# Batch 0 of a fused attention and max-out kernel reordered, its fill counted differently, its last tile split

## The chip, the cores and the metric

The kernel runs on one core of a Trainium2 chip. TensorE (PE) does matmuls and transposes into PSUM, ScalarE (ACT) and VectorE (DVE) read PSUM and write SBUF, GpSimd (POOL) works on SBUF and issues the loads that change type, SyncE (SP) issues plain loads and stores. Each engine works through its own instructions in the order in which the program names them. The metric is the device time of one execution in microseconds; lower is better.

## The reference

Blockwise causal attention, then a max-out layer:

```python
# q, k, v: [8 batches, 8 heads, 576, 64] float32; blocks of 64 positions
scores = scale * q @ k.transpose(0, 1, 3, 2)
scores = where(block_i >= block_j, scores, -1e9)      # block_i = pos // 64
attn = softmax(scores)                                # along the last axis
x = (attn @ v).transpose(0, 2, 1, 3).reshape(4608, 512)
g = maximum(x @ w1, x @ w2)                           # w1, w2: [512, 1024]
out = g @ w_out                                       # w_out: [1024, 512]
```

## The kernel before

The order of every engine's work is written out by hand (`manual_schedule`); a tile pool with `bufs=n` makes the (n+1)th tile wait until the first is done with.

*Attention.* The 64 heads are worked in 32 pairs, one per step `s`, four steps to a batch (`HP` = 4). Q and K come for two pairs at a time, as group `g` of 16: `load_qk` (float32, on SP's queue; group 0's K on ACT's), `cast` to bf16 on an engine that the call names, `transposes` on PE, and copies into `qT`, `kT`. With `gated=True` POOL first writes one column of the raw tile, and SP's load waits for that. A pair's scores come in two bursts. `burst_a` makes two PSUM tiles `u0`, `u1` and exps both on ACT, `burst_b` does so with `u2`, `u3`; the pool `ps_s` has two buffers, so `u2` waits for the exp of `u0`, and `u3` for that of `u1`. POOL zeroes the masked corners (`mask`). `av` multiplies a pair's exps with V and divides by the sums on DVE; a pair is 30 matmuls, 6 for row tiles 0 and 1 and 24 for 2 to 4. It runs `LAG` = 2 steps behind the scores. `x_out(g)` transposes the result of two pairs into `xT`; after a batch's second one `done_tokens` grows by 576.

*Max-out.* `xT` is taken in nine spans of 512 tokens. `h_unit` is 8 matmuls of 512 columns (four for w1, four for w2), a copy and a maximum on DVE; `y_unit` is 8 matmuls against `w_out`, a copy on ACT and a store on SP. They form one generator, `moe()`, of single matmuls. `fill(n)` takes the next n of them, as far as `done_tokens` allows: so they fill PE between the attention's steps. `fill_of(s)` spreads what is ready over the steps left until the batch after next:

```python
left = 10 - s if s < 10 else 4 - (s - 2) % 4
return -(-ready() // left)
```

`w1`, `w2`, `V` and `w_out` are loaded by POOL with a cast, through a queue of their own (q0 in the profile; SP's is q1).

*Order around the change.* In the main loop a step does: `n = fill_of(s)`; the `x_out` that is due; `burst_a`; part of the fill; the next group's transposes; `burst_b`; `pool_work(s)` (loads and casts ahead); `av(s - 2)` with fill between its parts; the rest of the fill. In steps 0 to 3 nothing is ready to fill, and `PLAN` puts `av(0)` at the end of step 2 and `av(1)`, `av(2)`, `av(3)` at the end of step 3. Step 4 first makes room for the transposes of group 2 and starts the fill.

Of the kernel before, what the change touches and what calls it, by code (L numbers as in the profile page):

```python
# [8 lines left out]
FP32 = mybir.dt.float32  # L9
# [5 lines left out]
def kernel(  # L15
# [10 lines left out]
    nc = tc.nc  # L26

    B, H, S, D = q.shape
    P = 128
    BLK = 64  # L30
    HP = H // 2
    NPAIR = B * HP
    d_model = H * D
    d_ff = moe_w1.shape[1]
    NDM = d_model // P
    NFF = d_ff // P
    NTOK = B * S
# [6 lines left out]
    RPP = S // NP  # L44
# [8 lines left out]
    NCH = 5  # L53
# [5 lines left out]
    ring = ctx.enter_context(tc.tile_pool(name="ring", bufs=1))  # L59
    small = ctx.enter_context(tc.tile_pool(name="small", bufs=4))  # L60
    xpool = ctx.enter_context(tc.tile_pool(name="xp", bufs=3))
    raw = ctx.enter_context(tc.tile_pool(name="raw", bufs=2))
    qkn = ctx.enter_context(tc.tile_pool(name="qkn", bufs=2))
    h1_pool = ctx.enter_context(tc.tile_pool(name="h1", bufs=3))
    g_pool = ctx.enter_context(tc.tile_pool(name="g", bufs=2))
# [23 lines left out]
    def load_qk(g, queues, gated=False):  # L89
        b, u = divmod(g, GPB)  # L90
        for nm, src, queue in (("q", q, queues[0]), ("k", k, queues[1])):
            raws[nm, g] = t = raw.tile([P, 2, RPP * D], FP32, name=f"{nm}raw")
            if gated:
                nc.gpsimd.memset(t[:, 0, :1], 0.0)
            queue.dma_start(
                out=t[:],
                in_=src[b, 4 * u:4 * u + 4].rearrange(
                    "(s h) (p t) d -> (h p) s (t d)", h=2, t=RPP),
            )

    def cast(nm, g, parts):
        t = raws.pop((nm, g)).rearrange("p s (t d) -> p t s d", d=D)
        qk_n[nm, g] = n = qkn.tile([P, RPP, 2, D], BF16, name=f"{nm}n")
        for copy, j0, j1 in parts:
            copy(out=n[:, j0:j1], in_=t[:, j0:j1])  # L105

    def load_v(b, c):
        rows = min(P, S - c * P)
        nc.gpsimd.dma_start(  # L109
            out=vv_r[b % NV][:rows, c, :, :D],  # L110
            in_=v[b, :, c * P:c * P + rows, :].rearrange("h p d -> p h d"),
        )
# [5 lines left out]
    def load_w(f0, fw):  # L118
        for dst, src in ((w1_sb, w1r), (w2_sb, w2r)):
            nc.gpsimd.dma_start(out=dst[:, :, f0:f0 + fw], in_=src[:, :, f0:f0 + fw])  # L120

    def load_wo(c0, n):
        nc.gpsimd.dma_start(out=wo_sb[:, c0:c0 + n, :], in_=wor[:, c0:c0 + n, :])
# [16 lines left out]
        nc.vector.memset(aT_r[r][BLK:, :, CB[4] + 512:], 0.0)  # L140
        nc.vector.memset(aT_r[r][:BLK, :, AW:], 0.0)
    cast("q", 0, ((dve, 0, 6), (pool, 6, RPP)))
    cast("k", 0, ((act, 0, 6), (pool, 6, RPP)))
    for c in range(3):
        load_v(0, c)
    cast("q", 1, ((pool, 0, RPP),))
    for c in range(3, NCH):
        load_v(0, c)
    load_w(0, 256)
    load_w(256, 256)  # L150

# [26 lines left out]
    def y_unit(i, s):  # L178
        g = g_tiles[i]
        t0 = i * SPAN + s * P  # L180
        py = ps_m.tile([P, d_model], FP32, name="ps_y", tag="m")
        for f in range(NFF):
            nc.tensor.matmul(  # L183
                py[:], g[:, f, s * P:(s + 1) * P], wo_sb[:, f, :],
                start=(f == 0), stop=(f == NFF - 1),
            )
            if f == NFF - 1:
                y = y_pool.tile([P, d_model], FP32, name="y")
                nc.scalar.copy(out=y[:], in_=py[:])  # L189
                nc.sync.dma_start(out=out[t0:t0 + P, :], in_=y[:])  # L190
            yield

    def moe():
        ny = SPAN // P
        for i in range(NSPAN):
            need = (i + 1) * SPAN
            for f in range(NFF):
                yield from ((need, 0) for _ in h_unit(i, f))
                if i > 1 and f % 2 == 0:
                    yield from ((need, 0) for _ in y_unit(i - 1, f // 2))  # L200
            if i == 0:
                for s in range(ny):
                    yield from ((need, 0) for _ in y_unit(0, s))
        for s in range(ny):
            yield from ((NTOK, 0) for _ in y_unit(NSPAN - 1, s))


    needs = []
    for i in range(NSPAN):
        needs += [(i + 1) * SPAN] * (2 * NDM * NFF + (SPAN // P * NFF if i != 1 else 0))  # L210
    needs += [NTOK] * (SPAN // P * NFF)
    moe_steps = moe()
    at = [0]

# [6 lines left out]
    def fill(n):  # L221
        for _ in range(min(n, ready())):
            next(moe_steps)
            at[0] += 1
# [4 lines left out]
    def transposes(nm, g, copies):  # L229
        n = qk_n.pop((nm, g))  # L230
        pts = [ps_m.tile([P, RPP, NP], BF16, name=f"ps_{nm}T", tag="m") for _ in range(2)]
        for j in range(RPP):
            for i in range(2):
                r = slice(i * NP, (i + 1) * NP)
                nc.tensor.transpose(  # L235
                    pts[i][:, j, :], n[r, j].rearrange("p s d -> p (s d)"), ident[r, r],
                )

        def copy_out():
            for i in range(2):  # L240
                t = (qT_r if nm == "q" else kT_r)[(2 * g + i) % NT]
                copies[i](  # L242
                    out=t[:, :S].rearrange("q (p j) -> q p j", j=RPP),
                    in_=pts[i].rearrange("q j p -> q p j"),
                )
        return copy_out
# [29 lines left out]
    def burst_b(p):  # L276
        u2 = ps_s.tile([P, 2, 512], FP32, name="ps_s", tag="s")
        scores(p, u2, 0, 2, 256, 320)
        scores(p, u2, 320, 3, 384, 192)
        u3 = ps_s.tile([P, 2, 512], FP32, name="ps_s", tag="s")  # L280
        scores(p, u3, 0, 4, 512, 64)
        exp(p, u2, 512, 1024)
        mask(p, 1024)
        mask(p, 1344)
        exp(p, u3, 64, 1536, m=BLK)
# [47 lines left out]


    LAG = 2
    PLAN = {0: [], 1: [], 2: [0], 3: [1, 2, 3], 4: [], 5: []}

    def fill_of(s):
        if s >= NPAIR - LAG:
            return 27  # L340
        left = 10 - s if s < 10 else 4 - (s - 2) % 4
        return -(-ready() // left)


    def pool_work(s):
        g, i = divmod(s, 2)
        if s == 0:
            load_qk(2, (SP, SP), gated=True)
            load_w(512, 512)
        elif s == 1:  # L350
            load_qk(3, (SP, SP), gated=True)
        elif s == 2:
            load_v(1, 0)
            load_v(1, 1)
        elif s == 3:
            load_v(1, 2)
            cast("q", 2, ((act, 0, RPP),))
            cast("k", 2, ((pool, 0, RPP),))
        elif s == 4:
            load_v(1, 3)  # L360
            load_v(1, 4)
            cast("q", 3, ((pool, 0, RPP),))
            cast("k", 3, ((pool, 0, RPP),))
            load_qk(4, (SP, SP))
        elif s == 5:
            load_wo(0, 4)
            load_wo(4, 4)
            cast("q", 4, ((pool, 0, RPP),))
        else:
            if i == 0 and g + 2 < NG:  # L370
                load_qk(g + 2, (SP, SP))
            if g + 1 + i < NG:
                cast("kq"[i], g + 1 + i, ((pool, 0, RPP),))
            nb, j = divmod(s + 2, HP)
            if nb < B:
                for c in ((0, 1), (2, 3), (4,), ())[j]:
                    load_v(nb, c)

    T_AT = {s: [("qk"[s % 2], s // 2 + 1)] for s in range(NPAIR - 2)}
    T_AT[2] = T_AT[3] = T_AT[4] = []  # L380
    T_AT[5] = [("q", 3), ("k", 3)]

    def t_pair(s):
        outs = [transposes(nm, g, (dve, dve if s < HP else act)) for nm, g in T_AT.get(s, [])]
        return lambda: [f() for f in outs]

    cq = transposes("q", 0, (dve, act))
    ck = transposes("k", 0, (act, dve))
    cq()
    ck()  # L390
    x_due = []
    for s in range(NPAIR):
        g, i = divmod(s, 2)
        avs = PLAN.get(s, [s - LAG])
        n = fill_of(s)
        if x_due:
            x_out(x_due.pop())
        if s == HP:
            n = fill_of(s)
            fill(6)  # L400
            cq = transposes("q", 2, (dve, act))
            ck = transposes("k", 2, (dve, act))
            cq()
            ck()
            fill(6)
        burst_a(s)
        if s == 0:
            cast("k", 1, ((dve, 0, RPP),))
        n_a = n // 2 if n > 12 else n * 2 // 5
        n_b = n // 6 if avs and s >= HP else 0  # L410
        fill(n_a)
        if s < HP:
            t_pair(s)()
            burst_b(s)
        else:
            copy_out = t_pair(s)
            burst_b(s)
            copy_out()
        pool_work(s)
        for p in avs:  # L420
            av(p, [0, 1])
            fill(n_b)
            av(p, [2, 3, 4])
            if p % 2:
                x_due.append(p // 2)
            if p == 2:
                x_out(x_due.pop())
        fill(n - n_a - n_b)
    for p in range(NPAIR - LAG, NPAIR):
        if x_due:  # L430
# [4 lines left out]
        fill(11)  # L435
    x_out(NG - 1)
    fill(len(needs))

# [29 lines left out]
```

## Time and profile before

| | |
|---|---|
| median of three runs | 304.68 us (304.28 to 305.38) |
| the profiled execution | 304.71 us, span 302.9 us |
| PE busy | 276.1 us, 91% of the span |
| DVE, ACT, POOL busy | 179.8, 138.4, 96.0 us |
| `h` matmuls (L165) | 576, mean 379 ns |
| `y` matmuls (L183) | 288, mean 379 ns |
| AV matmuls (L303) | 960, mean 198 ns |
| score matmuls (L252) | 384, mean 292 ns |
| exps (L258) | 128, mean 833 ns |

How to read the rows below. In a timeline a row has start and duration in us, engine, line, operation, tiles, shape, count, and in brackets how long the engine idled just before and what ended that. A row of stages has the stage, its length, then busy time and (instructions) of PE, PE's weight loads, DVE, ACT and POOL, the granted clock, the DMA share and GB/s. A group has line, engine, operation, tiles and shape, its count, then busy us, mean ns of one, and idle us before them with what ended it. A row of waits has who waited for whom, us in total, times, and the longest. A row of a DMA queue has packets, MB, and their time as a share of sixteen engines. Matmuls are pipelined, so their durations overlap.

### The profile page before, as it was taken

Reading aid. Unit: us, or ns where it says so; the run is one execution under the profiler, and the core shown is the slowest. Engines: PE = TensorE matmul, PEld = TensorE weight load, DVE = VectorE, ACT = ScalarE, POOL = GpSimd, SP = SyncE. Lnnn points to the kernel's source line nnn. Section 1 sums busy time; section 2 is a strip of 40 time slices with the busy share of each in tenths; the row PEclk is TensorE's granted clock in tenths of the full one; section 3 lists DMA queues with packets and bytes.
Section 4 is the critical chain, followed back from the end, with each engine's and each line's share of the span. In section 5 each row is a group of like instructions: output and inputs, shape, how many; then the busy total and the mean of one; then the engine's idle time right before and its main releaser. Section 6 shows DMA issues by size and latency. Waiting matters only on the chain.

```text
span 302.9 us, 7360 instructions
## 1 busy us (share of the span) xinstructions
PE 276.1 (91%) x3072; PEld 143.0 (47%) x3072; DVE 179.8 (59%) x359; ACT 138.4 (46%) x198; POOL 96.0 (32%) x216
## 2 busy tenths in 40 slices
PE   1577889998998999999998999899999999999994
PEld 1346334454455544554554545455444554444441
DVE  5535667545877665756565756676555866455530
ACT  3674457687446544574537535735534110100112
POOL 3973067645532623244325432453000000000000
PEclk9999999999999999999999999999999999999999
DMA  7999989997960675386717870584211011110103
GB/s 272 122 215 295 276 100 205 87 253 253 257 109 2 69 99 174 96 145 61 232 38 178 86 201 37 193 84 57 44 37 37 35 38 69 37 69 35 69 37 138
DMA packets 55649, 36.65 MB, mean 121 GB/s; under 512 B 38720, under 2 KB 42816, under 8 KB 55616
## 3 DMA queue, kind: packets, MB, share of 16 engines
q0 software_dynamic: 41728, 7.87, 31.8%
q1 hardware_dynamic: 13616, 27.73, 26.3%
q10 hardware_dynamic: 272, 0.59, 0.5%
q8 instruction: 24, 0.39, 0.5%
q14 instruction: 9, 0.07, 0.1%
HBM read 34.60 MB, written 9.44 MB: 145 GB/s over the span
## 4 chain that ended last, share of the span: by engine, by line
PE 82%; ACT 6%; DVE 3%; issue 3%; POOL 3%; DMA 2%; ACTq 0%
PE ps_h L165 40%; PE ps_y L183 20%; PE ps_o L303 11%; PE ps_s L252 7%; ACT aT L258 6%; PE ps_kT L235 2%; DMA qraw<-in_q_dram 2%; PE ps_xe L323 2%; POOL vv L109 1%; PE ps_qT L235 1%; DVE xp L310 1%; POOL qn L105 1%; DVE kT L242 1%; POOL kn L105 1%; ACT y L189 1%
## 5 line engine op out<-in xcount | busy, mean ns | idle before, releaser
L165 PE MATMUL ps_h<-xT,w_sb 128*128 128x512 bf16 x576 | 136.7, 379 | 0.9 <-DVE xT L329 0.4
L258 ACT ACTIVATE aT<-ps_s 128x1024 bf16<-128x1024 f32 (+1 forms) x128 | 98.8, 833 | 67.2 <-PE ps_s L252 66.2
L165 PEld LDWEIGHTS <-w_sb 128*128 128x128 bf16 x576 | 52.7, 98 | 61.3 <-issue 5.6
L172 DVE CAST h<-ps_h 128x512 bf16<-128x512 f32 x72 | 49.7, 690 | 49.9 <-PE ps_h L165 48.9
L183 PE MATMUL ps_y<-wo_sb,g 128*128 128x512 bf16 x288 | 69.4, 379 | 0.1
L263 POOL MEMSET aT<- 64x128 bf16 x128 | 23.3, 200 | 132.0 <-ACT aT L258 131.5
L189 ACT COPY y<-ps_y 128x512 f32<-128x512 f32 x36 | 21.1, 586 | 81.8 <-PE ps_y L183 56.3
L174 DVE TENSOR_TENSOR g<-h,ps_h 128x512 bf16<-128x512 bf16 x72 | 49.4, 686 | 11.7 <-PE ps_h L165 11.0
L252 PE MATMUL ps_s<-qT,kT 64*128 64x64 bf16 (+4 forms) x384 | 37.5, 292 | 10.6 <-ACT aT L258 9.9
L303 PE MATMUL ps_o<-vv,aT 128*128 128x65 bf16 x960 | 40.5, 198 | 0.9 <-ACT y L189 0.5
L183 PEld LDWEIGHTS <-g 128*128 128x128 bf16 x288 | 26.7, 98 | 30.0 <-issue 1.3
L303 PEld LDWEIGHTS <-aT 128*128 128x128 bf16 x960 | 35.5, 100 | 11.0 <-DVE xp L310 4.7
L109 POOL DMA_DIRECT2D vv<-in_v_dram x40 | 33.7, 848 | 0.0
L310 DVE TENSOR_TENSOR xp<-ps_o,rec 128x256 bf16<-128x256 f32 x64 | 31.4, 491 | 2.2
L252 PEld LDWEIGHTS <-kT 64*128 64x128 bf16 x384 | 17.7, 98 | 25.5 <-issue 19.3
L309 DVE RECIPROCAL rec<-ps_o 128x4 f32<-128x4 f32 x64 | 11.9, 186 | 27.5 <-PE ps_o L303 26.9
L242 DVE COPY kT<-ps_kT 128x576 bf16<-128x576 bf16 x17 | 12.7, 754 | 11.5 <-PE ps_kT L235 11.5
L105 POOL CAST qn<-qraw 128x1152 bf16<-128x1152 f32 (+1 forms) x15 | 17.0, 1134 | 5.3 <-DMA qraw<-in_q_dram 4.5
L105 POOL CAST kn<-kraw 128x1152 bf16<-128x1152 f32 (+1 forms) x15 | 16.6, 1106 | 2.2 <-DMA kraw<-in_k_dram 1.4
L235 PE MATMUL ps_qT<-ident,qn 64*128 64x64 bf16 x288 | 7.8, 196 | 8.3 <-DVE qn L105 6.4
L242 DVE COPY qT<-ps_qT 128x576 bf16<-128x576 bf16 x17 | 12.7, 752 | 4.3 <-PE ps_qT L235 4.1
L242 ACT COPY qT<-ps_qT 128x576 bf16<-128x576 bf16 x15 | 9.5, 632 | 7.1 <-PE ps_qT L235 7.1
(32 smaller groups left out, 83.9 us busy)
## 6 DMA issues: line engine op xcount, KB each, us to landing
qraw<-in_q_dram SPq DMA_DIRECT2D x16, 576.0 KB, 4.1
out_dram<-y SPq DMA_DIRECT2D x36, 256.0 KB, 2.0
kraw<-in_k_dram SPq DMA_DIRECT2D x15, 576.0 KB, 5.2
vv<-in_v_dram POOLq DMA_DIRECT2D x32, 128.0 KB, 4.5
w_sb<-in_moe_w_dram POOLq DMA_DIRECT2D x4, 256.0 KB, 6.4
w_sb<-in_moe_w_dram POOLq DMA_DIRECT2D x2, 512.0 KB, 16.3
wo_sb<-in_moe_w_out_dram POOLq DMA_DIRECT2D x2, 512.0 KB, 8.2
kraw<-in_k_dram ACTq DMA_DIRECT2D x1, 576.0 KB, 5.4
```

The source lines that it names most:

```text
L105: copy(out=n[:, j0:j1], in_=t[:, j0:j1])
L109: nc.gpsimd.dma_start(out=vv_r[b % NV][:rows, c, :, :D], in_=v[b, :, c * P:c * P + rows, :].rearrange("h p d -> p h d"),)
L165: nc.tensor.matmul(pt[:], w_sb[:, c, f * P:(f + 1) * P], xT[:, c, t0:t0 + SPAN], start=(c == 0), stop=(c == NDM - 1),)
L172: nc.vector.tensor_copy(out=h1[:], in_=pt[:])
L174: nc.vector.tensor_max(g[:, f, :], h1[:], pt[:])
L183: nc.tensor.matmul(py[:], g[:, f, s * P:(s + 1) * P], wo_sb[:, f, :], start=(f == 0), stop=(f == NFF - 1),)
L189: nc.scalar.copy(out=y[:], in_=py[:])
L242: copies[i](out=t[:, :S].rearrange("q (p j) -> q p j", j=RPP), in_=pts[i].rearrange("q j p -> q p j"),)
L252: nc.tensor.matmul(ps[:m, hh, col:col + w], kT[r, c * P:c * P + m], qT[r, q0:q0 + w], start=True, stop=True,)
L258: nc.scalar.activation(out=aT_r[p % NA][:m, :, a0:a0 + w], in_=ps[:m, :, :w], func=AF.Exp, scale=scale,)
L303: nc.tensor.matmul(po[:, gi, hh, :], a[:, hh, a0:a0 + P], vv[:, c, h0 + 2 * hh, :], start=(mm == 0), stop=(mm == n_mm - 1),)
L310: nc.vector.tensor_mul(xp[:, ts[0]:ts[0] + n, :, p % 2], po[:, :, :, :D], rec[:, :n].to_broadcast([P, n, 2, D]),)
```

## The change

- The raw pool of Q and K gets a third buffer. K of group 0 is cast by ACT (5 rows) and DVE (4), no longer partly by POOL. The copies of group 0's transposes go pair by pair.
- Group 2 is loaded behind V of batch 0, ahead of the first w loads, no longer in step 0.
- Steps 0 to 3 get a loop of their own: `burst_b` follows `burst_a` with nothing but `av(s - 2)`'s first part between; transposes of group 1 stand behind `burst_b` of steps 0 and 1; `av(0)` and `av(1)` lie in steps 2 and 3, `av(2)` and `av(3)` behind them.
- V of batch 1 and `w_out` are issued at the end of step 3 in one go; K of group 2 is cast on ACT instead of POOL; Q and K of group 3 are cast in step 3.
- From step 4 on `n = fill_of(s)` is counted behind `x_out`, and steps 4 and 5 split their fill in three as the others do.
- The last y tile is made in two halves of 256 columns; each half is copied by ACT and DVE, 128 columns each, and stored by ACT's and SP's queue.

```diff
-    raw = ctx.enter_context(tc.tile_pool(name="raw", bufs=2))
+    raw = ctx.enter_context(tc.tile_pool(name="raw", bufs=3))
...
-    cast("k", 0, ((act, 0, 6), (pool, 6, RPP)))
+    cast("k", 0, ((act, 0, 5), (dve, 5, RPP)))
...
     for c in range(3, NCH):
         load_v(0, c)
+    load_qk(2, (SP, SP), gated=True)
     load_w(0, 256)
     load_w(256, 256)
...
+    def y_last(i, s):
+        g = g_tiles[i]
+        t0 = i * SPAN + s * P
+        w = d_model // 2
+        for h in range(2):
+            py = ps_m.tile([P, w], FP32, name="ps_y", tag="m")
+            for f in range(NFF):
+                nc.tensor.matmul(
+                    py[:], g[:, f, s * P:(s + 1) * P], wo_sb[:, f, h * w:(h + 1) * w],
+                    start=(f == 0), stop=(f == NFF - 1),
+                )
+                if f == NFF - 1:
+                    for u, (copy, queue) in enumerate(((act, ACT), (dve, SP))):
+                        m = u * w // 2
+                        y = y_pool.tile([P, w // 2], FP32, name="yl")
+                        copy(out=y[:], in_=py[:, m:m + w // 2])
+                        queue.dma_start(
+                            out=out[t0:t0 + P, h * w + m:h * w + m + w // 2], in_=y[:])
+                yield
...
-        for s in range(ny):
+        for s in range(ny - 1):
             yield from ((NTOK, 0) for _ in y_unit(NSPAN - 1, s))
+        yield from ((NTOK, 0) for _ in y_last(NSPAN - 1, ny - 1))
...
-        def copy_out():
-            for i in range(2):
+        def copy_out(which=(0, 1)):
+            for i in which:
...
-    PLAN = {0: [], 1: [], 2: [0], 3: [1, 2, 3], 4: [], 5: []}
...
         if s == 0:
-            load_qk(2, (SP, SP), gated=True)
             load_w(512, 512)
         elif s == 1:
             load_qk(3, (SP, SP), gated=True)
         elif s == 2:
-            load_v(1, 0)
-            load_v(1, 1)
+            pass
         elif s == 3:
-            load_v(1, 2)
+            for c in range(NCH):
+                load_v(1, c)
+            load_wo(0, 4)
+            load_wo(4, 4)
             cast("q", 2, ((act, 0, RPP),))
-            cast("k", 2, ((pool, 0, RPP),))
-        elif s == 4:
-            load_v(1, 3)
-            load_v(1, 4)
+            cast("k", 2, ((act, 0, RPP),))
             cast("q", 3, ((pool, 0, RPP),))
             cast("k", 3, ((pool, 0, RPP),))
+        elif s == 4:
             load_qk(4, (SP, SP))
         elif s == 5:
-            load_wo(0, 4)
-            load_wo(4, 4)
             cast("q", 4, ((pool, 0, RPP),))
...
-    T_AT[2] = T_AT[3] = T_AT[4] = []
+    T_AT[0] = T_AT[1] = T_AT[2] = T_AT[3] = T_AT[4] = []
...
     cq = transposes("q", 0, (dve, act))
     ck = transposes("k", 0, (act, dve))
-    cq()
-    ck()
+    cq((0,))
+    ck((0,))
+    cq((1,))
+    ck((1,))
+    for s in range(HP):
+        burst_a(s)
+        if s == 0:
+            cast("k", 1, ((dve, 0, RPP),))
+        if s >= 2:
+            av(s - 2, [0, 1])
+        burst_b(s)
+        pool_work(s)
+        if s < 2:
+            transposes("qk"[s], 1, (dve, dve))()
+        else:
+            av(s - 2, [2, 3, 4])
+    for p in (2, 3):
+        av(p, [0, 1])
+        av(p, [2, 3, 4])
+        x_out(p - 2)
+
     x_due = []
-    for s in range(NPAIR):
+    for s in range(HP, NPAIR):
         g, i = divmod(s, 2)
-        avs = PLAN.get(s, [s - LAG])
-        n = fill_of(s)
         if x_due:
             x_out(x_due.pop())
+        n = fill_of(s)
         if s == HP:
-            n = fill_of(s)
             fill(6)
...
-        if s == 0:
-            cast("k", 1, ((dve, 0, RPP),))
         n_a = n // 2 if n > 12 else n * 2 // 5
-        n_b = n // 6 if avs and s >= HP else 0
+        n_b = n // 6
         fill(n_a)
-        if s < HP:
-            t_pair(s)()
-            burst_b(s)
-        else:
-            copy_out = t_pair(s)
-            burst_b(s)
-            copy_out()
+        copy_out = t_pair(s)
+        burst_b(s)
+        copy_out()
         pool_work(s)
-        for p in avs:
+        if s >= HP + LAG:
+            p = s - LAG
             av(p, [0, 1])
             fill(n_b)
             av(p, [2, 3, 4])
             if p % 2:
                 x_due.append(p // 2)
-            if p == 2:
-                x_out(x_due.pop())
+        else:
+            fill(n_b)
         fill(n - n_a - n_b)
```

More of the change, by code (lines that the diff above doesn't have):

```diff
@@ L210 @@
         needs += [(i + 1) * SPAN] * (2 * NDM * NFF + (SPAN // P * NFF if i != 1 else 0))
-    needs += [NTOK] * (SPAN // P * NFF)
+    needs += [NTOK] * ((SPAN // P + 1) * NFF)
     moe_steps = moe()
@@ L379 @@
     T_AT = {s: [("qk"[s % 2], s // 2 + 1)] for s in range(NPAIR - 2)}
-    T_AT[2] = T_AT[3] = T_AT[4] = []
+    T_AT[0] = T_AT[1] = T_AT[2] = T_AT[3] = T_AT[4] = []
     T_AT[5] = [("q", 3), ("k", 3)]
     def t_pair(s):
-        outs = [transposes(nm, g, (dve, dve if s < HP else act)) for nm, g in T_AT.get(s, [])]
+        outs = [transposes(nm, g, (dve, act)) for nm, g in T_AT.get(s, [])]
         return lambda: [f() for f in outs]
```

## The prediction, made before the change was built or run

> **What bounds the kernel now.** I read the page first (TensorE busy 91%, and 1, 5, 7, 7 tenths in its first four slices), then the matmul groups from 66 us on, for what PE waits for there.
>
> ```profile
> PE   1577889998998999999998999899999999999994
> ...
> L252 PE MATMUL ps_s<-qT,kT 64*128 64x64 bf16 x90 | 9.3, 190 | 2.6 <-ACT aT L258 2.6
> ...
> L252 PE MATMUL ps_s<-qT,kT 64*128 64x320 bf16 x46 | 7.0, 298 | 3.1 <-ACT aT L258 3.1
> ```
>
> From 66 us on PE idles 5.7 us ahead of the second burst's scores, for exps on ACT, and hardly elsewhere. Where, the stages tell: cut at each step's first score matmul, steps 14 and 15, then the step that opens the next group of four, and step 30.
>
> ```profile
> 94.66:98.34 3.68, 2.56 (x74) 1.91 (x68) 2.53 (x6) 3.14 (x5) 0.63 (x4) 1.00 0.02 4
> 98.34:107.78 9.44, 9.44 (x111) 4.79 (x110) 6.29 (x14) 4.61 (x7) 6.48 (x11) 1.00 0.56 59
> ...
> 126.67:130.35 3.68, 2.57 (x75) 1.91 (x68) 2.53 (x6) 3.14 (x5) 0.63 (x4) 1.00 0.98 319
> ...
> 222.69:230.87 8.18, 8.04 (x83) 3.89 (x75) 5.15 (x11) 3.59 (x5) 0.75 (x4) 1.00 0.13 47
> ```
>
> Step 14 has no fill: n is counted before x_out(5) frees the next tile, so it is 0, and steps 15 to 17 take 32 MoE matmuls each. In the full step PE never idles (16 and 17 are like it); in step 14 ACT is busy 3.14 of 3.68 us and PE idles 1.12. The timeline of step 14 shows it as two gaps, 0.59 and 0.52, each for an exp:
>
> ```profile
> 95.15 0.53 PE L235 MATMUL ps_qT<-ident,qn 64*128 64x64 bf16 x18
> 96.27 0.39 PE L252 MATMUL ps_s<-qT,kT 64*128 64x320 bf16 x4 [0.59 <-ACT aT L258]
> 97.19 0.21 PE L252 MATMUL ps_s<-qT,kT 64*128 64x64 bf16 x2 [0.52 <-ACT aT L258]
> ```
>
> Five steps are like this (10, 14, 18, 22, 26): 5 x 1.12 = 5.6 of the 5.7 us.
>
> The other loss is ahead of the first fill. The timeline of batch 0, its score bursts and what follows:
>
> ```profile
> 8.47 1.03 PE L252 MATMUL ps_s<-qT,kT 64*128 64x512 bf16 x6 [0.72 <-ACT kT L242]
> ...
> 13.33 1.04 PE L252 MATMUL ps_s<-qT,kT 64*128 64x512 bf16 x6 [1.06 <-ACT aT L258]
> ...
> 14.85 1.42 DVE L242 COPY kT<-ps_kT 128x576 bf16<-128x576 bf16 x2 [1.61 <-PE ps_kT L235]
> ...
> 16.88 1.04 PE L252 MATMUL ps_s<-qT,kT 64*128 64x512 bf16 x6 [0.68 <-ACT aT L258]
> ...
> 17.53 3.00 ACT L258 ACTIVATE aT<-ps_s 128x1024 bf16<-128x1024 f32 x4 [0.56 <-PE ps_s L252]
> ...
> 19.69 1.83 PE L303 MATMUL ps_o<-vv,aT 128*128 128x65 bf16 x30
> ...
> 21.45 1.03 PE L252 MATMUL ps_s<-qT,kT 64*128 64x512 bf16 x6
> ...
> 24.27 3.15 PE L303 MATMUL ps_o<-vv,aT 128*128 128x65 bf16 x60
> ...
> 28.30 0.91 PE L303 MATMUL ps_o<-vv,aT 128*128 128x65 bf16 x24 [0.20 <-DVE xp L310]
> ...
> 31.12 0.41 DVE L329 COPY xT<-ps_xo 128x512 bf16<-128x512 bf16 x1
> 31.58 1.02 PE L165 MATMUL ps_h<-xT,w_sb 128*128 128x512 bf16 x4 [0.37 <-DVE xT L329]
> ```
>
> Bursts start at 8.47, 13.33, 16.88, 21.45; x is whole at 31.53. An AV matmul, less 0.19 for the last one's own time, takes (1.83 - 0.19)/30 = 55 ns at 19.69 and (0.91 - 0.19)/24 = 30 at 28.30: PE runs at about half pace until some 27 us, though the page's clock strip shows full speed from the start.
>
> **The change, part by part.**
>
> *Fill counted with x in.* 96 matmuls go as 24 in each of four steps instead of 0, 32, 32, 32 (steps 10 to 13: 16 each instead of 0, 22, 21, 21). With n = 24, 12 stand between the two bursts, 12 x 0.216 = 2.6 us (from 1.90 us for 8, less the last one's tail, in the rows below), over the 1.12 waited; with 16 it is 8, 1.7 us. The exps stay covered, ACT (4.61 of 9.44 us) and DVE (6.29) have room: up to 5.6 us gained. What is late next: fill now starts right behind x_out, while DVE still copies x. Step 30 does that already:
>
> ```profile
> 223.27 2.20 PE L165 MATMUL ps_h<-xT,w_sb 128*128 128x512 bf16 x8
> 223.55 0.41 DVE L329 COPY xT<-ps_xo 128x512 bf16<-128x512 bf16 x1
> ...
> 36.08 1.90 PE L165 MATMUL ps_h<-xT,w_sb 128*128 128x512 bf16 x8
> ```
>
> Eight matmuls take 2.20 instead of 1.90: 0.30 waited, five times 1.5. Net 5.6 - 1.5 = **-4.1 us**, bounds -5.6 (no wait) and -3.0 (half of the gap comes back).
>
> *V1 and w_out at batch 0's end, K2 cast on ACT, Q3/K3 cast on POOL right after.* In step 5 PE waits for POOL's late casts, which stand behind V issues:
>
> ```profile
> 40.10:46.52 6.42, 5.22 (x63) 2.28 (x63) 3.81 (x6) 3.83 (x6) 4.64 (x9) 1.00 0.94 171
> ...
> PE ps_kT L235 <- POOL kn L105: 0.7, 1, 0.7
> PE ps_qT L235 <- POOL qn L105: 0.3, 1, 0.3
> PE ps_h L165 <- DVE kT L242: 0.3, 1, 0.3
> ```
>
> Idle is 1.20. The page's groups and the timeline have the prices of POOL's issues and casts:
>
> ```profile
> L109 POOL DMA_DIRECT2D vv<-in_v_dram x40 | 33.7, 848 | 0.0
> L105 POOL CAST qn<-qraw 128x1152 bf16<-128x1152 f32 (+1 forms) x15 | 17.0, 1134 | 5.3 <-DMA qraw<-in_q_dram 4.5
> ...
> 46.01 1.50 POOL L123 DMA_DIRECT2D wo_sb<-in_moe_w_out_dram x2
> ```
>
> After, POOL issues five V1 loads (5 x 0.85) and two of w_out (1.5) from some 25 us, then two casts (2.3), done at about 33; their transposes stand near 42. The two POOL waits go, the DVE one stays: **-1.0 us**, bounds -1.2 and 0. ACT's extra cast (1.1, as on POOL) follows the last exps, while PE, DVE and the next exps are held by x; without that cover it would cost its 1.1. Behind POOL's 5.8 us of issues stand only step 4's masks, needed two steps later. fill(n_b) in steps 4 and 5 moves fill inside a full step: 0.
>
> *Bursts close up.* K0's split and the new copy order: scores still wait for K0's transposes and one copy, so the start stays at 8.45. Step 0: Q1's transposes no longer stand ahead of burst_b, so step 1 starts when the third exp frees its buffer: 9.1 + 3 x 1.0 = 12.15 (was 13.33). Step 1: its last scores come at 14.85; K1's transposes (0.66) and first copy (0.75) stand behind them, so burst 2 starts at 16.6, not 15.8 (was 16.88): the copy is late next. Step 2: with six AVs in a gap (0.36), the last scores at 19.3, then 24 AVs at 55 ns, burst 3 starts at 20.9 (was 21.45). Its last scores run to 23.85, against 24.33. Behind them stand 24 + 30 AVs up to the end of AV 2: 23.85 + 54 x 0.055 = 26.85, where it was 24.27 + 3.15 = 27.42. From there to a whole x it was 4.1 (31.53 - 27.42), for x_out(0), AV 3 and x_out(1), whose divisions and copies follow one another on DVE; with AV 3 partly at the slow pace I take 4.3, so 31.2 against 31.53: **-0.4 us**, bounds +0.5 (K1's copy later still) and -2.2 (fast pace early, below). V0 keeps its place in POOL's queue and is issued 0.4 earlier.
>
> *Third raw buffer, load 2 early.* SP is now held only by the two gates: load 2 at about 12.3 (was 16.40), 3 at 16.4, 4 right behind, 5 as soon as load 2 is cast, near 26. POOL's w loads are behind it on the same DMA engines. The DMA answers for 15 to 20 and 21 to 32 us:
>
> ```profile
> q0 software_dynamic: 1660, 0.83, 128.3%
> ...
> q1 hardware_dynamic: 1034, 2.26, 59.5%
> q0 software_dynamic: 1049, 0.99, 53.5%
> ```
>
> Alone, POOL's queue moves 332 packets per us; beside SP's, 95 against 94. Loads 2 to 5 are 2048 packets (2.3 KB each), 22 us at 94: 15 to 37. The first halves of w (2048 packets of 0.5 KB) then end near 36.5, the second (1024) by 42. Fill first needs f = 2 near 37 and the second half near 41 and 43.5: just in time. **0**. The upper bound is +2.5: if SP's packets share from some 13.7 on, V0's last 600 or so take 6 us instead of 1, AV 0 waits for them about 1 us, and w comes 1.5 later; the lower is 0. I take 0, because in the first of those answers SP had issued at 16.4 (the timeline's row below) and its queue moved nothing until 20: what POOL had queued went first.
>
> ```profile
> 16.40 0.37 SPq L95 DMA_DIRECT2D qraw<-in_q_dram  x1
> ```
>
> The Trainium skill, "DMA: Bandwidth & Descriptors", Queues, rings and completion order, has each DMA engine go round its queues packet by packet; the second answer agrees, the first does not, and by the rule alone the sum would carry the +2.5, 301.2.
>
> *Last y tile in halves.*
>
> ```profile
> 299.14 0.59 ACT L189 COPY y<-ps_y 128x512 f32<-128x512 f32 x1 [1.14 <-PE ps_y L183]
> 299.75 0.33 SPq L190 DMA_DIRECT2D out_dram<-y  x1
> ```
>
> Sixteen 256-column matmuls stream what eight of 512 do. Behind the last one stands a copy of 128 columns, about 0.27 (ACT's 64x128 exp in the groups takes 0.262) instead of 0.59, and half the data: -0.25 of the transfer, an estimate. ACT's own issue may cost 0.1 more. **-0.5 us**, bounds -0.8 and 0.
>
> ```profile
> L258 ACT ACTIVATE aT<-ps_s 64x128 bf16<-64x128 f32 x32 | 8.4, 262 | 0.0
> ```
>
> **Sum.** -4.1 - 1.0 - 0.4 + 0 - 0.5 = -6.0. The profiled execution took 304.71 (span 302.9), the median of the runs is 304.68: 298.7.
>
> **Rivals.**
> 1. *Fast pace early.* The stretch of 3.41 us just ahead of 27 has PE busy 3.11, the one before it 2.72, and the pace doubles after the first:
>
> ```profile
> 20.22:23.63 3.41, 2.72 (x34) 1.00 1.19 295
> 23.63:27.04 3.41, 3.11 (x59) 1.00 1.13 296
> ```
>
> Packed steps 2 and 3 idle about 0.85 in 4.3, so a stretch as full as 3.11 can fall near 19 to 22.5. Then the AVs left run at 30 ns (54 x 25 ns = 1.35) and burst 3 closes 0.5 sooner: -1.8, 296.9. Against: the stretch from 20.22 was nearly as full and didn't do it.
>    The Trainium skill, "TensorE: Matmul & The Clock Gate", Part 1, states that the array runs at half clock until a window of about 3.4 us was busy, and that the windows run freely; the two paces agree, and by it this rival is a matter of phase.
> 2. *POOL held up.* With w's second half, V1 and w_out issued while w's first half still flows, some 7000 packets are queued at once by these rates, where before it was some 3700; if there is a limit between, POOL's issues block until w drains near 42; Q3/K3's casts then end near 46 against 42.5 needed: +3.7, and the -1.0 is lost: 303.4. Against: POOL's V issues take 0.85 in the mean whatever is queued. The milder form, w late by 2.5, gives 301.2.
> 3. *SP's loads starve w: slower.* Fill's first tile (f = 0, 1) is 1024 packets of w, needed at about 30.3. If POOL's queue got 30 packets per us beside SP's instead of 95, 660 would be there at 37 and the tile at 39: +8.7, 307.4. It decides where the tile lands after 37.3, below some 47 packets per us. Against: 95 in the trace, and SP's loads waiting rather than leading at 16.4.
> 4. *The regrouping does nothing:* the wait for x takes the whole 1.12 each time: 298.7 + 4.1 = 302.8. Against: step 30's 0.30.
>
> **How the numbers follow.** Forecast 0.58, rival 1 0.16, 2 0.14 (mild form most of it), 3 0.05, 4 0.07. The forecast's own range is 297.3 to 300.2; with rival 1 below and mild 2 above it becomes 295.8 to 301.3, leaving 3, 4 and the hard form of 2 out. Within 0.3% (about 0.9 us, what a measurement here can tell from no change): only mixtures of 2 and 4, 0.04; slower 0.05; faster 0.91.
>
> **What would show it.** Right: no step without fill from 10 to 29; L252's idle for ACT from 66 us on falls from 5.7 to under 1; a wait of about 0.3 for the x copies at steps 10, 14, 18, 22, 26; no PE wait for POOL in step 5; bursts at about 8.4, 12.2, 16.6, 20.9, x near 31; a last copy of about 0.27. Wrong: PE waiting for a DMA of w or V between 30 and 48 us, POOL issues over 1 us, AV at 55 ns past 29 us, or steps of 24 fills longer than 24 x 0.216 + 2.5 = 7.7 us.

## The result, and the profile after

The changed kernel takes 296.76 us (median; 296.26 to 297.99), the kernel before 304.48: 7.7 us less, ratio 0.9752 (95% interval 0.971 to 0.9794). Forecast were 298.7 and 295.8 to 301.3. The profiled execution took 296.26, its span is 294.5, against 302.9 before. Cut at the same points, the two spans differ as follows (step starts are those of the first score matmul):

| stretch | before, us | after, us | difference | forecast |
|---|---|---|---|---|
| up to the start of step 4 | 35.54 | 33.39 | -2.15 | -0.4 |
| steps 4 to 9 | 33.80 | 33.66 | -0.14 | -1.0 |
| steps 10 to 29 | 153.35 | 147.82 | -5.53 | -4.1 |
| step 30 to the end of the last matmul | 76.37 | 76.39 | 0 | 0 |
| from there to the end of the span | 3.87 | 3.20 | -0.67 | -0.5 |

The mean step from 10 to 29 fell by 0.28 us; that is the bulk. Stages of the changed kernel, steps 14 to 17 (length, then busy us and instructions of PE, weight loads, DVE, ACT and POOL, clock, DMA):

```profile
91.74:99.74 8.00, 7.39 (x96) 3.87 (x91) 5.52 (x11) 4.12 (x6) 2.69 (x6) 1.00 0.05 20
99.74:107.45 7.71, 7.66 (x100) 4.03 (x102) 4.92 (x10) 4.12 (x6) 3.83 (x9) 1.00 0.67 82
107.45:114.95 7.50, 7.39 (x96) 3.87 (x91) 5.38 (x11) 4.13 (x6) 3.15 (x7) 1.00 1.07 215
114.95:122.67 7.72, 7.67 (x101) 4.04 (x102) 4.92 (x10) 4.12 (x6) 1.89 (x5) 1.00 0.29 58
```

Four like steps stand where 3.68, 9.44, 9.41 and 9.48 stood. Taking off 24 x 0.216 = 5.18 us of fill, the rest of a step is 2.82, 2.53, 2.32 and 2.54; steps 15 and 17 hold an x_out, step 14 the wait for x. Per group of four the saving isn't the same: 0.62 us in steps 10 to 13, 1.08 in 14 to 17, and 1.27 in each of the three later groups. The score matmuls no longer wait for ACT (groups, from 60 us on):

```profile
L274 PE MATMUL ps_s<-qT,kT 64*128 64x64 bf16 x92 | 9.4, 189 | 0.0
...
L274 PE MATMUL ps_s<-qT,kT 64*128 64x320 bf16 x46 | 6.9, 298 | 0.0
```

The timeline of batch 0:

```profile
8.36 1.03 PE L274 MATMUL ps_s<-qT,kT 64*128 64x512 bf16 x6 [0.73 <-ACT kT L264]
...
11.91 1.03 PE L274 MATMUL ps_s<-qT,kT 64*128 64x512 bf16 x6 [0.20 <-ACT aT L280]
...
15.27 1.42 DVE L264 COPY kT<-ps_kT 128x576 bf16<-128x576 bf16 x2 [2.13 <-PE ps_kT L257]
...
16.09 1.03 PE L274 MATMUL ps_s<-qT,kT 64*128 64x512 bf16 x6 [0.82 <-DVE kT L264]
...
20.33 1.03 PE L274 MATMUL ps_s<-qT,kT 64*128 64x512 bf16 x6
...
23.11 1.81 PE L325 MATMUL ps_o<-vv,aT 128*128 128x65 bf16 x54
...
28.96 0.41 DVE L351 COPY xT<-ps_xo 128x512 bf16<-128x512 bf16 x1
29.43 1.02 PE L166 MATMUL ps_h<-xT,w_sb 128*128 128x512 bf16 x4 [0.59 <-DVE xT L351]
```

Bursts start at 8.4, 11.9, 16.1 and 20.3 (forecast 8.4, 12.2, 16.6, 20.9); burst 2 waits 0.82 for K1's copy, as foreseen. The 54 AVs at 23.11 take 30 ns each: PE is already at its fast pace, 4 us earlier than before. x is whole at 29.37 instead of 31.53.

POOL and what PE waits for between 37 and 45 us:

```profile
29.88 0.69 POOL L109 DMA_DIRECT2D vv<-in_v_dram  x1 [2.18 <-DMA w_sb<-in_moe_w_dram]
...
34.38 0.76 POOL L123 DMA_DIRECT2D wo_sb<-in_moe_w_out_dram  x1 [3.82 <-DMA w_sb<-in_moe_w_dram]
...
40.25 1.15 POOL L105 CAST kn<-kraw 128x1152 bf16<-128x1152 f32 x1
...
PE ps_kT L257 <- POOL kn L105: 0.7, 1, 0.7
PE ps_h L166 <- DVE kT L264: 0.6, 1, 0.6
PE ps_qT L257 <- POOL qn L105: 0.2, 1, 0.2
```

POOL's issues block, and the casts, forecast to end at 33, end at 41.4: PE's wait in step 5 is as long as before (1.5 us against 1.3). The trace names the semaphore of each POOL load: eight take turns, and each load waits for the landing of the one eight before it. The fifth load of V1 is the sixteenth, and waits for the third of w; the second of w_out, issued only at 38.4, for the first big one. In the kernel before these landings were long past when their turn came.

The loads of w themselves land 4 to 9 us later, as reckoned, since SP's queue now runs beside them (medians from issue to landing; before 6.4 and 16.3):

```profile
w_sb<-in_moe_w_dram POOLq DMA_DIRECT2D x4, 256.0 KB, 14.2
w_sb<-in_moe_w_dram POOLq DMA_DIRECT2D x2, 512.0 KB, 23.3
```

The tail has the two short copies:

```profile
291.30 0.27 ACT L209 COPY yl<-ps_y 128x128 f32<-128x128 f32 x1 [0.61 <-PE ps_y L201]
291.59 0.34 ACTq L210 DMA_DIRECT2D out_dram<-yl  x1
291.59 0.29 DVE L209 COPY yl<-ps_y 128x128 f32<-128x128 f32 x1 [0.58 <-ACT yl L209]
```

DVE's copy stands behind ACT's, not beside it: from the end of the last matmul to the end of the last copy it is 0.62 us instead of 0.67. Nearly all of the 0.67 saved lies behind the copies; the last store takes 1.57 us from issue to landing instead of 2.03.

### The profile page after: what moved, and what is told of

The parts are those of the page before. It is cut to its first block, busy times and chain, and to the rows that moved or that the text cites. A ratio compares the mean times of both kernels' runs of the same rounds, so it can differ in the third digit from the quotient of the medians.

```text
span 294.5 us, 7341 instructions
## 1 busy us (share of the span) xinstructions
PE 270.1 (92%) x3033; PEld 141.1 (48%) x3080; DVE 182.6 (62%) x362; ACT 138.4 (47%) x200; POOL 94.4 (32%) x214
## 3 DMA queue, kind: packets, MB, share of 16 engines
HBM read 34.60 MB, written 9.44 MB: 150 GB/s over the span
## 4 chain that ended last, share of the span: by engine, by line
PE 82%; DVE 8%; ACT 5%; issue 2%; DMA 2%; POOL 1%; POOLq 0%; ACTq 0%; DVEq 0%
PE ps_h L166 41%; PE ps_y L184 19%; PE ps_o L325 10%; PE ps_s L274 7%; ACT aT L280 4%; DVE g L175 2%; PE ps_kT L257 2%; DMA qraw<-in_q_dram 2%; PE ps_qT L257 2%; DVE kT L264 1%; DVE xp L332 1%; PE ps_xe L345 1%; DVE xT L350 1%; DVE xT L351 1%; PE ps_y L201 1%
## 5 line engine op out<-in xcount | busy, mean ns | idle before, releaser
L166 PE MATMUL ps_h<-xT,w_sb 128*128 128x512 bf16 x543 | 133.4, 380 | 4.3 <-DVE xT L351 2.6
L166 PEld LDWEIGHTS <-w_sb 128*128 128x128 bf16 x576 | 51.8, 98 | 61.9 <-issue 9.2
L184 PE MATMUL ps_y<-wo_sb,g 128*128 128x512 bf16 x266 | 66.6, 379 | 1.1 <-DVE kT L264 0.3
L274 PE MATMUL ps_s<-qT,kT 64*128 64x64 bf16 (+4 forms) x384 | 36.7, 291 | 4.9 <-ACT aT L280 3.3
L184 PEld LDWEIGHTS <-g 128*128 128x128 bf16 x280 | 25.6, 98 | 27.3 <-issue 0.4
L331 DVE RECIPROCAL rec<-ps_o 128x4 f32<-128x4 f32 x64 | 11.8, 185 | 26.9 <-PE ps_o L325 26.7
L274 PEld LDWEIGHTS <-kT 64*128 64x128 bf16 x384 | 16.9, 97 | 20.6 <-issue 13.7
L105 POOL CAST kn<-kraw 128x1152 bf16<-128x1152 f32 x13 | 14.9, 1147 | 0.8
```

The source lines that it names most:

```text
L166: nc.tensor.matmul(pt[:], w_sb[:, c, f * P:(f + 1) * P], xT[:, c, t0:t0 + SPAN], start=(c == 0), stop=(c == NDM - 1),)
L184: nc.tensor.matmul(py[:], g[:, f, s * P:(s + 1) * P], wo_sb[:, f, :], start=(f == 0), stop=(f == NFF - 1),)
L274: nc.tensor.matmul(ps[:m, hh, col:col + w], kT[r, c * P:c * P + m], qT[r, q0:q0 + w], start=True, stop=True,)
```

## The experiments

Three put one part each into the kernel before; the others start from the changed kernel.

**The counting alone.**

```diff
-        n = fill_of(s)
         if x_due:
             x_out(x_due.pop())
+        n = fill_of(s)
```

> The kernel before with one edit: n = fill_of(s) is counted behind x_out. Theory A (the prediction's term): 5 x (1.12 idle gained less 0.30 waited for x) = -4.1 us, about 300.5. Theory B (read from the two traces): a step without fill costs 3.68 where a step of 24 costs its fill and 2.3 to 2.6, so -5.5 us, about 299.1. Both: no idle of the score matmuls for ACT from 66 us on, five waits of about 0.4 for the x copies. If the regrouping only works together with the new front: under 2 us.

Measured: 298.80 us against 304.82, ratio 0.9803 (0.9778 to 0.9827): -6.0. In its trace steps 10 to 29 take 147.83, as in the changed kernel to 0.01. Theory B holds, and the part stands alone. The wait for x is there: by the starts of the matmuls 0.10 in step 10, 0.50 in step 14 and 0.31 in steps 18, 22 and 26, together the 1.5 that the prediction had; in the timeline of step 14:

```profile
94.88 0.60 PE L165 MATMUL ps_h<-xT,w_sb 128*128 128x512 bf16 x2
95.82 1.45 PE L165 MATMUL ps_h<-xT,w_sb 128*128 128x512 bf16 x6 [0.34 <-DVE xT L329]
```

So the other term was too small: a step without fill cost not its 1.12 us of idle but about 3.68 - 2.32 = 1.36. Five times that less the waits is 5.3 us of the 5.5.

**The bursts alone** (steps 0 to 3 in their own loop, group 0's copies pair by pair, the fill of steps 4 and 5 split in three; loads, casts, counting and last tile as before).

```diff
+    for s in range(HP):
+        burst_a(s)
...
+        if s >= 2:
+            av(s - 2, [0, 1])
+        burst_b(s)
+        pool_work(s)
+        if s < 2:
+            transposes("qk"[s], 1, (dve, dve))()
+        else:
+            av(s - 2, [2, 3, 4])
```

> The kernel before with the new loop of steps 0 to 3 alone (loads, casts, counting and last tile as before). Theory A (the prediction's term): the closed bursts themselves bring 0.4 us, about 304.2, with x whole near 31.2. Theory B: they also let TensorE reach its fast pace earlier, as in the trace of the changed kernel (AV at 30 ns from about 23 us on instead of 27): x whole near 29.4, -2.1 us, about 302.5; how much depends on where the busy stretch falls, so the single executions spread by some 1.5 us.

Measured: 303.55, ratio 0.9962 (0.9948 to 0.9976): -1.3, between the two theories. In the profiled execution x is whole at 29.46 with PE fast from 21.2, but PE then falls back to the slow pace for one stretch, 28.05 to 31.46, and step 4 starts at 34.36.

**The last tile alone** (`y_last` in the kernel before).

> The kernel before with the last y tile in column halves alone. Theory A: from the end of the last matmul to the end of the span 3.2 us instead of 3.9, -0.6 us, about 304.2. Theory B: the halves cost as much in matmuls and weight loads as they save: 304.8.

Measured: 304.11, ratio 0.9982 (0.9974 to 0.9991): -0.55. The last matmul ends at 298.87 of a span of 302.07: 3.20 us, theory A. The three parts add to -6.0 - 1.3 - 0.55 = -7.9, the whole change measured -7.7.

**Casts ahead of V1 and w_out.**

```diff
         elif s == 3:
+            cast("q", 2, ((act, 0, RPP),))
+            cast("k", 2, ((act, 0, RPP),))
+            cast("q", 3, ((pool, 0, RPP),))
+            cast("k", 3, ((pool, 0, RPP),))
             for c in range(NCH):
                 load_v(1, c)
             load_wo(0, 4)
             load_wo(4, 4)
-            cast("q", 2, ((act, 0, RPP),))
-            cast("k", 2, ((act, 0, RPP),))
-            cast("q", 3, ((pool, 0, RPP),))
-            cast("k", 3, ((pool, 0, RPP),))
```

> The changed kernel, with the casts of Q and K of group 3 put ahead of the loads of V1 and w_out in POOL's queue in step 3. Theory A: POOL's loads go round eight completion semaphores, each load waits for the landing of the one eight before it, and that holds the casts until 41 us and costs PE 1.3 us in step 5; with the casts ahead, step 5 takes about 5.1 instead of 6.34 and the kernel 1.2 us less than the changed one, about 295.5. Theory B: the wait in step 5 is that of the transposes' own buffers: no change, 296.8.

Measured: 296.85, ratio 0.9742 (0.972 to 0.9763): no change from the changed kernel; in the profiled execution x is whole 0.8 us later, at 30.19, since PE's fast pace comes late there (see the changed kernel again, below). The casts end at 28.4, yet step 5 takes 6.09 instead of 6.34. What PE waits for there:

```profile
PE ps_kT L257 <- DVE qT L264: 0.8, 1, 0.8
PE ps_h L166 <- DVE kT L264: 0.3, 1, 0.3
```

Theory B: the transposes of Q and K make four PSUM tiles in one step, the pool has four, and K's wait for Q's to be copied out. The casts were one of two reasons for the same wait. Two runs below that leave the casts behind the loads (x_out early, and PE kept busy) have 6.09 in step 5 too.

**The early loads taken back** (two raw buffers, group 2 loaded in step 0).

```diff
-    raw = ctx.enter_context(tc.tile_pool(name="raw", bufs=3))
+    raw = ctx.enter_context(tc.tile_pool(name="raw", bufs=2))
...
-    load_qk(2, (SP, SP), gated=True)
     load_w(0, 256)
...
         if s == 0:
+            load_qk(2, (SP, SP), gated=True)
             load_w(512, 512)
```

> The changed kernel with two raw buffers, and group 2 loaded in step 0 as before. Theory A: SP's loads sent ahead share the DMA engines packet for packet with w, which lands 6 to 10 us later than before, and through the eight semaphores that holds POOL; with the loads late the third and fourth w load land near 21 and 23 instead of 30 and 34, POOL's casts end near 34 instead of 41, and the PE wait in step 5 goes: -1.2 us against the changed kernel, about 295.5. Theory B: the early loads are worth something themselves (Q2 in time): slower than the changed kernel by 0.5 to 2 us.

Measured: 296.77, ratio 0.9734 (0.971 to 0.9758): no change. w lands as before (6.9 and 17.2 us), V1's loads are issued without a wait, the casts end at 34: theory A's mechanism. Step 5 is 6.09 again, so its price falls as in the last run. The third buffer and the early loads are worth nothing here.

**Q of group 3 transposed in step 4** (with the casts ahead).

```diff
-    T_AT[5] = [("q", 3), ("k", 3)]
+    T_AT[4] = [("q", 3)]
+    T_AT[5] = [("k", 3)]
```

> The changed kernel with the casts ahead of the loads, and group 3's Q transposed in step 4, K in step 5, instead of both in step 5. Theory A: with POOL's wait gone, step 5 still waits 1.1 us for the PSUM buffers of four transposes at once (0.8 + 0.3 in the trace with the casts ahead); split, steps 4 and 5 together take about 0.9 less: 295.6. Theory B: the second copies then hold the scores of the step: no change, 296.6.

Measured: 295.44, ratio 0.9703 (0.9687 to 0.9719), 1.4 under the casts alone (1.2 by the ratios). Steps 4 and 5 take 4.82 and 4.39, together 9.21 instead of 10.65. Only the wait of step 4's own transposes is left between 30 and 46 us:

```profile
PE ps_kT L257 <- ACT qT L264: 0.6, 1, 0.6
```

**x_out early.**

```diff
             if p % 2:
-                x_due.append(p // 2)
+                fill(n - n_a - n_b - 3)
+                x_out(p // 2)
+                fill(3)
+            else:
+                fill(n - n_a - n_b)
         else:
             fill(n_b)
-        fill(n - n_a - n_b)
+            fill(n - n_a - n_b)
```

> The changed kernel, with x_out put ahead of the last three fill matmuls of the step before instead of at the step's start. Theory A: the five waits for the x copies (2.0 us of PE idle in the trace) go, -1.5 us, about 295.2. Theory B: the transposes then wait for the divisions on DVE instead, no gain: 296.8.

Measured: 299.02, ratio 0.9798 (0.9776 to 0.9821): 2.3 slower than the changed kernel. Steps 4 to 9 grow from 33.4 (the runs above) to 34.78, steps 10 to 29 from 147.82 to 148.99. In step 7 only two fill matmuls stand between the last AV and x_out, and its transposes wait for the division:

```profile
55.16 0.59 PE L184 MATMUL ps_y<-wo_sb,g 128*128 128x512 bf16 x2
55.69 0.20 PE L345 MATMUL ps_xe<-ident,xp 64*128 64x64 bf16 x1
...
56.21 0.20 PE L345 MATMUL ps_xe<-ident,xp 64*128 64x64 bf16 x1 [0.29 <-DVE xp L332]
```

The starts stand 0.48 apart there. Theory B, and worse than it said. With 24 fills a step the early place gains about what it loses.

**The changed kernel again.**

> The changed kernel again, on this chip beside the others. Theory A: x whole at 29.4 when TensorE is fast from about 22.5, and at 30.2 to 30.4 when only from about 27, which is a matter of where the stretches fall in an execution; 296 to 297.5, executions spread by a good 1 us. Theory B: the early fast pace belongs to the kernel: x whole at 29.4 again in the profiled execution.

Measured: 296.91 (296.54 to 298.19), ratio 0.9756 (0.9737 to 0.9776). x is whole at 29.5 with PE fast from 22.8: theory B for batch 0. But in this execution PE lost its pace later, in one stretch of 3.41 us behind the wait in step 5 (stages as above; the clock is the column behind POOL):

```profile
39.82:43.23 3.41, 1.76 (x45) 0.98 (x44) 2.11 (x4) 1.17 (x2) 2.83 (x8) 1.00 2.67 143
43.23:46.64 3.41, 3.40 (x12) 0.98 (x11) 1.24 (x2) 1.79 (x5) 1.49 (x3) 0.50 1.64 191
46.64:50.05 3.41, 3.36 (x52) 1.82 (x52) 2.42 (x5) 2.76 (x3) 0.40 (x2) 1.00 0.67 111
```

Clock 0.50, 12 matmuls where the changed kernel's first profile has 19 (42.97 to 46.38): steps 5 and 6 take 7.82 and 5.71 instead of 6.34 and 5.35, 1.8 us. In the casts-first run, whose bursts stand as far apart, PE was fast only from 26.9 and x whole at 30.2. So theory A holds for the size, and the early pace isn't certain: of the six profiled executions with this batch 0 and no unread matmuls, three had it by 22.8 and three only from 26.9 or later.

Which stretches bring the fast pace? The changed kernel at 15.66 to 22.49, then the casts-first run at 16.64 to 26.88:

```profile
15.66:19.07 3.41, 2.43 (x22) 1.29 (x23) 1.64 (x4) 2.33 (x3) 2.77 (x11) 1.00 1.14 271
19.07:22.49 3.42, 3.17 (x40) 2.17 (x39) 1.36 (x4) 2.17 (x4) 0.54 (x3) 1.00 1.32 241
...
16.64:20.05 3.41, 2.86 (x38) 2.17 (x36) 0.61 (x2) 2.88 (x4) 1.86 (x11) 1.00 1.19 281
20.05:23.47 3.42, 2.87 (x32) 1.66 (x30) 1.36 (x4) 2.71 (x3) 0.40 (x2) 1.00 1.29 266
23.47:26.88 3.41, 3.41 (x71) 3.23 (x69) 2.00 (x7) 2.38 (x4) 1.48 (x3) 1.00 1.17 313
```

The fast pace begins behind the stretches with 3.17 and 3.41 busy, not behind 2.43 or 2.87; the column of the clock shows 1.00 throughout, for want of a record before its first change. The same work cut at another place gives 3.17 or two of 2.86: a matter of phase.

**PE kept busy while it waits for the first data** (matmuls of the identity that nobody reads).

```diff
+    def spin(n):
+        pt = ps_m.tile([P, P], FP32, name="ps_w", tag="m")
+        for _ in range(n):
+            nc.tensor.matmul(pt[:], ident[:], ident[:], start=True, stop=True)
+
+    spin(42)
     cq = transposes("q", 0, (dve, act))
...
     ck((1,))
+    spin(3)
     for s in range(HP):
         burst_a(s)
         if s == 0:
+            spin(5)
```

> The changed kernel with 50 matmuls of the identity that nobody reads, while TensorE waits for the first loads (42), for the first copies (3) and for the first exps (5). Theory A: TensorE goes to its fast pace after a busy stretch of 3.4 us and keeps it as long as no such stretch is idle; it is then fast from 8 us or earlier, transposes and scores of batch 0 take half, bursts stand 3.2 to 3.3 us apart, x is whole near 27.5 instead of 29.4: -1.5 us, about 295.2, and the executions spread less. Theory B: the pace falls back in the gaps of batch 0: no change or slower by 0.3.

Measured: 296.25, ratio 0.973 (0.9709 to 0.9751), 0.5 under the changed kernel's median and within both spreads. PE is fast from 4.28 and slow again from 11.10 to 24.76, x whole at 29.4. Theory B: the pace falls back although the longest gap ahead of it is 0.85 us, behind two stretches little more than 0.6 busy:

```profile
4.28:7.69 3.41, 2.14 (x56) 1.71 (x53) 2.96 (x10) 1.21 (x2) 2.17 (x3) 1.00 1.04 406
7.69:11.10 3.41, 2.06 (x38) 1.17 (x37) 2.14 (x3) 3.41 (x6) 3.41 (x5) 1.00 1.67 156
11.10:14.51 3.41, 2.28 (x30) 1.23 (x29) 1.13 (x2) 2.85 (x5) 3.41 (x7) 0.50 1.52 106
```

**Three at once:** the casts ahead, x_out early, and the unread matmuls of the last run, with their edits as above.

> The changed kernel with all three: casts ahead of the loads, x_out early, the 50 unread matmuls. If the parts add up: -1.2 - 1.5 - 1.5 = -4.2 us against the changed kernel, about 292.6. If POOL's casts then wait for the load of group 3 (it lands near 27), the first part brings less: about 293.5.

Measured: 298.08, ratio 0.9784 (0.9764 to 0.9803): 1.3 slower than the changed kernel. Step 4 starts at 33.0 and the last score matmul at 228.3, 195.3 us later; with x_out early alone these are 34.4 and 229.7, the same distance. So the loss is that of the place of x_out, the casts bring nothing beside it, and what the front saves doesn't make up for it.

**Every gap of batch 0 filled** (with the casts ahead; 137 unread matmuls, `idle()` stands between u2 and u3).

```diff
-    def burst_b(p):
+    def burst_b(p, idle=lambda: None):
...
+        idle()
...
+    spin(42)
...
+    spin(3)
...
         if s >= 2:
             av(s - 2, [0, 1])
-        burst_b(s)
+            spin(6)
+        else:
+            spin(9)
+        burst_b(s, lambda: spin(8))
...
             transposes("qk"[s], 1, (dve, dve))()
+            spin(6)
...
         av(p, [2, 3, 4])
+        spin(9)
         x_out(p - 2)
```

> The changed kernel with the casts ahead of the loads, and unread matmuls of the identity in every gap of batch 0 (42 before the first data, 6 to 9 in each gap between bursts and in each wait for DVE). Theory A: TensorE goes fast after a stretch of 3.4 us that is at least some 0.9 busy and falls back when one is only 0.6 busy; with the gaps filled it is fast from 8 us at the latest and stays so, batch 0 is then paced by the exps, x is whole near 27 instead of 29.4 to 30.4 and the kernel at about 294.5. Theory B: filling gaps delays the scores behind them by as much as it gains: 296.5 or more.

Measured: 294.37, ratio 0.9667 (0.9651 to 0.9683), with executions from 294.32 to 294.49, a spread of 0.2 us where the changed kernel has 1.7: theory A for the time. Its rule for the pace is not borne out: in this trace PE is fast from 4.25, behind a stretch 2.88 of 3.41 us busy, and stays so behind the next, which is 2.12 busy. The timeline:

```profile
7.91 0.61 PE L274 MATMUL ps_s<-qT,kT 64*128 64x512 bf16 x6
...
11.25 0.61 PE L274 MATMUL ps_s<-qT,kT 64*128 64x512 bf16 x6
...
14.97 0.61 PE L274 MATMUL ps_s<-qT,kT 64*128 64x512 bf16 x6 [0.39 <-DVE kT L264]
...
18.36 0.61 PE L274 MATMUL ps_s<-qT,kT 64*128 64x512 bf16 x6
...
26.77 0.41 DVE L352 COPY xT<-ps_xo 128x512 bf16<-128x512 bf16 x1
```

Six score matmuls take 0.61 instead of 1.03 from the first burst on, and x is whole at 27.2.

**Gaps filled, casts ahead, Q split.**

> The gaps of batch 0 filled with unread matmuls, casts ahead of the loads, and group 3's Q transposed in step 4. Theory A: the parts add up: filled gaps brought 2.5 us against the changed kernel, the split 1.4 against the casts alone; step 5 of the former took 6.78, 0.5 of it a wait for w, which stays: 294.4 - 1.4 = 293.0. Theory B: with x whole at 27 already, w's landings (30 and 34 for the third and fourth load) become the limit of steps 4 and 5: 294.

Measured: 294.26, ratio 0.9656 (0.9629 to 0.9683): no better than the gaps alone. Theory B. With x at 27.6 PE reaches w's later parts before they have landed (waits from 25 to 48 us; with the gaps alone this wait is 0.5):

```profile
PE ps_h L166 <- DMA w_sb<-in_moe_w_dram: 1.7, 2, 0.9
```

This and the run with the gaps alone beat the changed kernel by some 2.5 us. The late loads in place of the third buffer would bring w sooner; with the gaps filled that wasn't tried.

## Why the prediction was right, and where it was off

*Fill counted with x in:* right in mechanism, too small: -5.5 instead of -4.1. The step that failed is the price of a step without fill, taken as its two gaps (1.12). Comparing step lengths, 3.68 against the 2.32 that attention takes in a full step without x_out, gives 1.36, a mean: the groups of four saved from 0.62 to 1.27. In the starved step PE shows 2.56 us busy, more than those 2.32. Since the ends of matmuls are modelled, a short run that ends in a wait may look longer there than it costs inside a full stream; no run tests that. The wait for x, 1.5 in all, was right.

*V1, w_out and the casts:* -1.0 forecast, -0.1 measured. Two steps failed. POOL's issues were taken as never blocked; they are, by the semaphores, so rival 2 was right that POOL is held up, though not by a limit on queued packets. And the POOL waits were taken to vanish, where the wait for the four PSUM tiles stood right behind them: the casts-first run shows 0.25 us for the casts, the split 1.4 for the tiles. Rival 2's price of +3.7 was too high, since the casts ended at 41.4, not 46.

*Bursts:* -0.4 forecast; -2.15 in the profiled execution, about -1.2 where the fast pace comes late (x at 30.2 to 30.4), -1.3 measured for the part alone. The step that failed is the pace taken for the AVs behind the last burst: 55 ns each, where the profile has 30. Where that pace does come late, as the forecast had it, the last burst starts at 20.1 to 20.3 instead of 20.9, some 0.6 us of the rest. All starts were right within that, always on the slow side, and the wait for K1's copy was foreseen. Rival 1 (fast pace early, 296.9) has the mechanism that both profiled executions of the changed kernel show, and the weight given to it, 0.16, looks too low: with the bursts packed, four of seven executions without unread matmuls had the early pace.

*Early loads:* nothing, as forecast; w lands 4 to 9 us later, in time as long as x isn't earlier. SP's packets, which in the trace before stood back for 4 us, began after some 2 us here, and between 34 and 35 us SP's queue moved 96 packets beside 95 of POOL's. The Trainium skill, "DMA: Bandwidth & Descriptors", Queues, rings and completion order, has each DMA engine go round its queues packet by packet. The counts at 34 us agree, the first 2 us do not. V0 was in time none the less.

*Last tile:* -0.5 forecast, -0.67 measured, and near by luck. The shorter copy, forecast at -0.3, gave 0.05, because two copies stand one behind the other. What lies behind the copies, forecast at -0.25 less 0.1 for an issue and read from no row, gave 0.6, most of it in the last store (1.57 us instead of 2.03).

In the profiled execution the terms' errors, -1.4 for the fill, -1.8 for the bursts and -0.2 for the tail one way, +0.9 for the casts the other, partly cancel: 298.7 forecast, 296.26 there, 296.76 in the median. The median lies below the forecast's own range (297.3 to 300.2), and inside the stated one because rival 1 was mixed in. That rival 1's 296.9 meets it is luck too: its sum has the fill at -4.1 and the casts at -1.0. Of the prediction's signs of being wrong two came: POOL held for 2.2 and 3.8 us ahead of an issue, and steps of 24 fills longer than 7.7 us, 7.80 and 8.00 where they open a group, by the wait for x that the sum had.

## What to carry to other kernels

Fill work that hides a latency is worth most spread evenly: count what is ready after everything that makes it ready. Price a starved step by its length against a full step's, not by the idle that the trace shows in it. Before moving loads together, look for what their issue waits for (here the landing of the eighth load back), and before crediting a vanished wait, look for the next one on the same instruction.

## What the runs showed of the hardware

The record of PE's clock changes at distances of 3.41 us and multiples of it: 6.83 and 13.65 us in the run with 50 unread matmuls, 20.48 and 3.41 in the changed kernel's second profile. Cut at these times, the stretch ahead of the fast pace is mostly 3.07 to 3.41 us busy, while 2.72, 2.86 and 2.87 didn't bring it. But the busy share alone doesn't decide: in the run with 50 unread matmuls the first of these stretches brought the fast pace (its clock column has no record yet) and the second did not:

```profile
0.87:4.28 3.41, 2.91 (x28) 2.92 (x29) 2.24 (x13) 1.49 (x2) 0.37 (x2) 1.00 0.69 228
17.93:21.35 3.42, 3.08 (x38) 2.17 (x38) 0.93 (x3) 2.17 (x5) 0.67 (x4) 0.50 1.34 239
```

The pace can be lost without a long gap: behind stretches of 1.76, 2.02, 2.06 and 2.14 us busy, with no gap over 0.65 us in them, but it was kept behind the following two, the first from the run with every gap filled, the second from the changed kernel:

```profile
4.25:7.66 3.41, 2.12 (x55) 1.68 (x54) 2.96 (x11) 1.17 (x2) 2.13 (x3) 1.00 1.04 405
...
25.90:29.32 3.42, 1.87 (x43) 1.40 (x45) 2.85 (x9) 0.17 (x1) 1.80 (x3) 1.00 1.16 309
```

What decides in either direction stays open. The Trainium skill, "TensorE: Matmul & The Clock Gate", Part 1, states a window of about 3.4 us and that an idle one throttles. These runs agree with the window, and lost the pace in stretches more than half busy. A lost stretch cost 1.8 us in the changed kernel's second profile and some 0.9 with the bursts alone (from x whole to step 4 4.90 us instead of 4.01); the changed kernel's executions spread by 1.7.
